# A softmax-plus-feed-forward kernel: two output tiles finished before either is copied, two batches' states transposed by TensorE at the start, and one batch's M sessions moved up

## The chip, the cores and the metric

The kernel runs on one core of one Trainium2 chip. The metric is device time in microseconds (us) of one execution, lower is better. TensorE is called PE below, VectorE DVE, ScalarE ACT, GpSimd POOL and SyncE SP.

## What is computed

There are 8 batches, each with 8 heads, 512 tokens and 32 state rows, and 64 elements per head. An attention goes both ways between tokens and state, and its result goes through a feed-forward layer:

```
B, H, S, Ns, D = 8, 8, 512, 32, 64          # x: B,H,S,D   state: B,H,Ns,D
scores  = x @ state^T / sqrt(D);   a  = softmax(scores);    xread = a  @ state
scores2 = state @ x^T / sqrt(D);   a2 = softmax(scores2);   sread = a2 @ x
rows = concat([xread, sread], axis=2) -> transposed to (B * 544, 512)
h = rows @ w_in                       # 512 x 2048
out = max(0.01 * h, h) @ w_out        # 2048 x 512, result 4352 x 512, float32
```

## The kernel before, in words

The order of instructions on every engine is written out by hand: what the program says in order is what each engine runs in order, and an instruction that waits holds all that stand behind it on its engine. SP's queue is one such order too: it issues loads, stores and the transposing DMAs.

**The work of one batch.** `xread @ w_in` is not formed in two steps. The kernel multiplies the state with `w_in` first (`a_m`, line 334: "M sessions", four per batch, each for 512 of the 2048 columns; `m_evict`, lines 346 and 348, copies a session from PSUM into the bf16 tile `M`) and then multiplies the probabilities `aT` with `M` (`ff1`, line 355, 16 steps of two matmuls, each followed by the leaky ReLU on ACT, line 360, into `hT`). The second layer is cut into "pieces" (`piece`, line 383): a piece is four of the 16 matmuls that make an output tile of 128 tokens. Four pieces (`jq` 0 to 3) finish a tile, and there are four tiles (`i`) to a batch. The last piece is followed by a copy out of PSUM into `ysb` (line 389) and a store on SP's queue (line 395).

**The attention of one batch.** `a_scores` (line 213) makes the scores in PSUM (tag `sc`). `a_shift` (DVE, lines 223 to 233) finds the maximum over the 32 state rows and gives `sh`; `a_exp` (ACT, line 240) the exponentials; `a_probs` (DVE, lines 245 to 255) the sums, reciprocals and `aT`. `a_max2`, `a_exp2`, `a_probs2` (lines 273 to 292) do the other softmax, over tokens, and `a_a2t` transposes its result by a DMA on SP (line 299), which `a_sread` (line 307) needs.

**Transposes.** PE needs x and state with the head's elements on partitions. x of batches 0 to 2 is transposed by PE (lines 434 and 193), later batches by a DMA (`a_xt_dma`, line 185). The states of batches 0 and 1 are transposed at the start by eight small matmuls against an identity (`state01`, line 146). Those of batches 2 to 7 are loaded by eight DMAs (`load_state`, line 165), cast by POOL (line 171) and transposed by one DMA (line 172).

**The stretch around the change.** Batch 0 is the start: its loads, scores, M sessions and ff1 are written out one by one. `spin` runs matmuls on zeros. Then comes batch 0's second layer (lines 612 to 642), and between its pieces stands all that batch 1 needs before its own ff1: the transposes of x (lines 616 to 619), scores, M sessions 1 to 3, both softmaxes. Tiles 0 and 1 lie in two PSUM banks of their own (tag `py`); tiles 2 and 3 share one PSUM tile of two banks, `wide` (named `pyw`). Tiles 2 and 3 are finished here, tiles 0 and 1 in the first steps of batch 1's ff1. After that a loop of 16 steps `s` (line 655) runs batch 1's ff1 with pieces between, and holds batch 2's attention; a second loop (line 688) does batches 2 to 7 in the same manner, each with the next batch's attention inside.

PSUM tiles are handed out by tag; a tag's next user waits until the last reader of the tile before is done. DMAs on SP share eight counters in turn, so each waits for the one eight places before it.

Of the kernel before, what the change touches and what calls it, by code (L numbers as in the profile page):

```python
# [9 lines left out]
P = 128  # L10
# [17 lines left out]
def kernel(  # L28
# [34 lines left out]
    xv = x[0].rearrange("h (p t) d -> p h (t d)", t=NT)  # L63
    for u in range(2):
        nc.sync.dma_start(xf[u][:], xv[:, NK * u:NK * (u + 1)])
    idle = consts.tile([P, S], BF16, name="idle")
    nc.vector.memset(idle[:], 0.0)
    warm = consts.tile([P, 2], FP32, name="warm")
# [58 lines left out]
    def spin(n, tag):  # L127
        p = psum.tile([P, S], FP32, name="pspin", tag=tag, bufs=2 if tag in ("ph", "py") else 1)
        for _ in range(n):
            nc.tensor.matmul(p[:], lhsT=idle[:, :P], rhs=idle[:], start=True, stop=True)  # L130
# [3 lines left out]

    stbd = consts.tile([P, NK, 2, NS], BF16, name="stbd")
    st1 = consts.tile([P, P], BF16, name="st1")
    st_t = consts.tile([P, B - 2, P], BF16, name="st_t")
    sr_t = consts.tile([P, NK, B * NS], BF16, name="sr_t")

    stb0 = consts.tile([P, 4, D], BF16, name="stb0")  # L140
# [15 lines left out]
            ps[:, :, D:].rearrange("p r (k q) -> p k q r", q=8),  # L156
        )

    stf = consts.tile([P, B - 2, P], FP32, name="stf")
    stb = consts.tile([P, B - 2, P], BF16, name="stb")  # L160

    def load_state():
        for k in range(NK):
            for g in range(2):
                nc.sync.dma_start(
                    stf[NS * k:NS * (k + 1), :, D * g:D * (g + 1)],
                    state[2:, 2 * k + g].rearrange("b n d -> n b d"),
                )

    def state_t():  # L170
        POO(stb[:], stf[:])
        nc.sync.dma_start_transpose(st_t[:], stb[:].rearrange("p b q -> p (b q)"))
# [30 lines left out]
    def st_of(a, g, k):  # L203
        rows = slice(D * g, D * (g + 1))
        if a.b == 0:
            return stbd[rows, k, g ^ (k // 2), :]
        return (st1 if a.b == 1 else st_t[:, a.b - 2])[rows, NS * k:NS * (k + 1)]

    def a_scores(a):
        sc = psum.tile([P, 2, S], FP32, name="sc", tag="sc", bufs=1)  # L210
        for k in range(NK):
            for g in range(2):
                nc.tensor.matmul(  # L213
                    sc[NS * k:NS * (k + 1), g, :],
                    lhsT=st_of(a, g, k),
                    rhs=a.xT[D * g:D * (g + 1), :, k, :],
                    start=True, stop=True,
                )
        a.sc = sc
# [44 lines left out]
    def a_exp(a):  # L264
        a.e1 = block_exp(a.sh, NB)
# [76 lines left out]
    def m_evict(a, c, pm, copy):  # L342
        cols = slice(DM * c, DM * (c + 1))
        if isinstance(pm, list):
            for g in range(2):
                copy(a.M[:, g, cols], pm[g][:])  # L346
        else:
            copy(a.M[:, :, cols], pm[:])  # L348
# [28 lines left out]
    def piece(b, hT, i, jq, bank=None, copy=SCA):  # L377
        if jq == 0:
            y = ys[b, i] = Y()
            y.py = psum.tile([P, DM], FP32, name="py", tag="py")[:] if bank is None else bank  # L380
        y = ys[b, i]
        for j in range(4 * jq, 4 * jq + 4):
            nc.tensor.matmul(  # L383
                y.py, lhsT=hT[:, j, P * i:P * (i + 1)], rhs=w_out_bf[:, j, :],
                start=(j == 0), stop=(j == 15),
            )
        if jq == 3:
            ysb = ypool.tile([P, DM], FP32, name="ysb", tag="ysb")
            copy(ysb[:], y.py)  # L389
            if b == B:  # L390
                for bb in range(4):
                    r0 = (4 * i + bb) * SROW + S
                    nc.sync.dma_start(out[r0:r0 + NS, :], ysb[NS * bb:NS * (bb + 1), :])  # L393
            else:
                nc.sync.dma_start(rows_of(b)[i], ysb[:])

    def rows_of(b):
        return out[b * SROW:b * SROW + S, :].rearrange("(p t) f -> t p f", t=NT)
# [40 lines left out]
    def xt0_evict(u, pxt, copies):  # L439
        for v, copy in enumerate(copies):  # L440
            copy(a0.xT[:, :, 2 * u + v, :], pxt[v][:])
# [16 lines left out]
    def rows0(u):  # L458
        scn[u] = psum.tile([P, S], FP32, name="scn", tag="ph")
        for c in range(NK):  # L460
            nc.tensor.matmul(
                scn[u][NS * c:NS * (c + 1), :], lhsT=stbd[:, 2 * u + c // 2, c % 2, :],
                rhs=a0.xT[:, :, 2 * u + c // 2, :], start=True, stop=False,
            )
# [70 lines left out]
    pxt = x0_half(1)  # L535
    m = max0(0)
    xt0_evict(1, pxt, (SCA, VEC))
    rows0(0)
    m = split0(m)
    scores0(1)  # L540
# [1 line left out]
    rows0(1)  # L542
    spread0(scn[0], m[0], False)
    exp0(0)
    spin(2, "py")
    spread0(scn[1], split0(m[1]), False)
    exp0(1)
    sum0(0)
# [63 lines left out]
    for i in (0, 1):  # L612
        piece(0, h0, i, 0)
    wide = psum.tile([P, 2, DM], FP32, name="pyw", tag="big", bufs=1)
    piece(0, h0, 2, 0, bank=wide[:, 0])
    for t0, copy in ((0, VEC), (2, SCA)):
        ps = psum.tile([P, 2, NK, P], BF16, name="pxt2", tag="ph")
        a_xt_pe(a1, ps, t0, t0 + 2)
        copy(a1.xT[:, t0:t0 + 2], ps[:])
    piece(0, h0, 3, 0, bank=wide[:, 1])  # L620
    nc.vector.memset(stf[:, 0, D - 1:D + 1], 0.0)
    load_state()
    a_scores(a1)
    m_evict(a1, 1, a_m(a1, 1, "ph"), SCA)
    a_shift(a1)
    a_max2(a1)
    for i in range(NT):
        piece(0, h0, i, 1)
        if i in (1, 3):
            c = 2 + i // 2  # L630
            m_evict(a1, c, a_m(a1, c, "ph"), SCA)
    a_exp(a1)
    for g in range(2):
        a_exp2(a1, g)
    a_probs(a1)
    state_t()
    open_xb(2)
    cast_x(2, 0, 8, SCA)
    for i in range(NT):
        piece(0, h0, i, 2)  # L640
    for i in (2, 3):
        piece(0, h0, i, 3, copy=VEC)
    a_probs2(a0)
    a_a2t(a0)
    a_probs2(a1)
    a_a2t(a1)
    a_open(a2, 2)


# [5 lines left out]
    for s in range(16):  # L655
        ff1(a1, h1, s)
        if s % 2:
            pb, hT, i, jq = fill[s // 2]
            piece(pb, hT, i, jq, copy=VEC if s == 3 else SCA)
        if s == 2:  # L660
            a_xt_full(a2)
            VEC(a2.xT[:], a2.pxt[:])
        elif s == 4:
            a_scores(a2)
            m_evict(a2, 0, a_m(a2, 0, "big"), SCA)
            a_shift(a2)
            a_max2(a2)
            cast_x(3, 0, 8, POO)
        elif s == 8:
            a_exp(a2)  # L670
        elif s == 9:
            a_sread(a0)
        elif s in (10, 11):
            a_exp2(a2, s - 10)
            if s == 11:
                a_probs(a2)
                a_probs2(a2)
        elif s == 13:
            pm = [a_m(a2, 1, "big"), a_m(a2, 2, "sc")]
            m_evict(a2, 1, pm[0], VEC)  # L680
            m_evict(a2, 2, pm[1], SCA)
            a_open(att_of[3], 3)
            a_xt_dma(att_of[3])
# [4 lines left out]
    for b in range(2, B):  # L688
        hT = hpool.tile([P, 16, S], BF16, name="hT", tag="hT")
        a = att_of[b]  # L690
        nxt = att_of[b + 1] if b + 1 < B else None
        order = [(b - 1, i, 3) for i in range(2)]
        order += [(b - 1, i, jq) for i in range(2, NT) for jq in range(4)]
        order += [(b, i, jq) for jq in range(3) for i in range(2)]
        for s in range(16):
            ff1(a, hT, s)
            if s == 0:
                if b + 2 < B:
                    load_x(b + 2, nc.sync)
                    open_xb(b + 2)  # L700
                a_a2t(a)
            elif s == 1:
                if nxt is not None:
                    a_scores(nxt)
                m_evict(a, 3, a_m(a, 3, "big"), SCA)
                if nxt is not None:
                    a_shift(nxt)
                    a_max2(nxt)
                if b + 2 < B:
                    cast_x(b + 2, 0, 8, POO)  # L710
            elif s == 6:
                if b == 2:
                    a_sread(a1)
            elif s == 8:
                a_sread(a)
            if nxt is not None:
                if s == 5:
                    a_exp(nxt)
                elif s in (6, 7):
                    a_exp2(nxt, s - 6)  # L720
                    if s == 7:
                        a_probs(nxt)
                        a_probs2(nxt)
                elif s == 10:
                    pm0 = a_m(nxt, 0, "big")
                    pm2 = a_m(nxt, 2, "phpy")
                    pm1 = a_m(nxt, 1, "sc")
                    m_evict(nxt, 2, pm2, VEC)
                    m_evict(nxt, 0, pm0, VEC)
                    m_evict(nxt, 1, pm1, SCA)  # L730
                if s == 13 and b + 2 < B:
                    a_open(att_of[b + 2], b + 2)
                    a_xt_dma(att_of[b + 2])
            pb, i, jq = order[s]
            piece(pb, hT if pb == b else h_prev, i, jq)
        h_prev = hT
# [48 lines left out]
```

## Time and profile before

| | us |
|---|---|
| median of three timed runs | 220.35 (220.31, 220.35, 222.07) |
| profiled execution: time | 222.05 |
| profiled execution: span from first to last instruction | 220.2 |

| engine | busy us | share of span |
|---|---|---|
| PE (matmul) | 211.4 | 96% |
| ACT | 139.3 | 63% |
| DVE | 100.2 | 45% |
| PE weight loads (beside matmuls) | 98.9 | 45% |
| POOL | 22.3 | 10% |

The profile is of one execution. Its page gives the busy time of each engine, the span in 40 slices, a chain of waits from the end backwards, and groups of instructions by line; the trace behind it gives every instruction with start, length and what ended the idle time before it. "Lnnn" is a line of the kernel before. The mean granted PE clock is 0.992 of full speed. The granted clock of a stretch is part of its row in a table of windows.

### The profile page before, as it was taken

How to read it: one execution, taken by the hardware profiler on the slowest of the kernel's cores; microseconds unless marked ns; L12 is line 12 of the kernel's file. 1: busy time of each engine (PE TensorE's matmuls, PEld its weight loads, DVE VectorE, ACT ScalarE, POOL GpSimd, SP SyncE). 2: the span in 40 equal slices, each digit the busy share in tenths (PEclk: the TensorE clock that was granted, in tenths of full speed). 3: DMA queues.
4: the chain of work that ended last, by engine and by line, in shares of the span. 5: the costliest groups of instructions: out<-in, count | busy, mean ns of one | idle time of the engine just before them, and what ended most of it. 6: DMA issues, size and time to landing. Idle time of an engine off the chain costs nothing.

```text
span 220.2 us, 3735 instructions
## 1 busy us (share of the span) xinstructions
PE 211.4 (96%) x1524; PEld 98.9 (45%) x1524; DVE 100.2 (45%) x152; ACT 139.3 (63%) x261; POOL 22.3 (10%) x36
## 2 busy tenths in 40 slices
PE   7999995999999999999999999999999999999993
PEld 2533432444345444444444444444444445466653
DVE  1676388489696607670667146733674000000000
ACT  3469757378869647874778477857685665554420
POOL 8820201003030003000300030000000000000000
PEclk9999999699999999999999999999999999999999
DMA  5999993695931395139512951181114111111113
GB/s 188 218 206 293 207 288 37 163 224 169 271 119 48 86 259 135 48 79 246 153 41 59 233 151 47 68 172 51 48 48 98 44 52 48 51 40 55 48 44 102
DMA packets 37632, 27.17 MB, mean 123 GB/s; under 512 B 22256, under 2 KB 32880, under 8 KB 37616
## 3 DMA queue, kind: packets, MB, share of 16 engines
q1 hardware_dynamic: 32704, 20.52, 35.6%
q0 software_dynamic: 4768, 6.29, 14.2%
q8 instruction: 12, 0.20, 0.4%
q10 hardware_dynamic: 144, 0.13, 0.3%
q14 instruction: 4, 0.03, 0.1%
HBM read 17.30 MB, written 8.91 MB: 119 GB/s over the span
## 4 chain that ended last, share of the span: by engine, by line
PE 78%; DMA 10%; ACT 4%; SPq 2%; DVE 2%; POOL 1%; issue 1%; ACTq 0%; POOLq 0%
PE py L383 46%; PE ph L355 22%; DMA xl<-in_x_dram 7%; PE pm L334 3%; PE ph L366 3%; DMA xf<-in_x_dram 3%; SPq L393 2%; PE psr L307 1%; PE pyw L383 1%; PE sc L213 1%; ACT hT L360 1%; ACT e L240 1%; PE pxt L193 1%; DMA out_dram<-ysb 1%; DVE qb L254 1%; DVE r L245 1%
## 5 line engine op out<-in xcount | busy, mean ns | idle before, releaser
L383 PE MATMUL py<-w_out_bf,hT 128*128 128x512 bf16 x464 | 119.4, 381 | 0.0
L360 ACT ACTIVATE hT<-ph 128x512 bf16<-128x512 f32 x112 | 67.0, 601 | 45.5 <-PE ph L355 45.5
L383 PEld LDWEIGHTS <-hT 128*128 128x128 bf16 x496 | 47.0, 98 | 61.0 <-issue 9.5
L355 PE MATMUL ph<-aT,M 128*128 128x512 bf16 x224 | 66.8, 384 | 0.3 <-ACT hT L360 0.3
L355 PEld LDWEIGHTS <-M 128*128 128x128 bf16 x224 | 21.8, 99 | 27.5 <-issue 2.7
L389 ACT COPY ysb<-py 128x512 f32<-128x512 f32 x30 | 17.6, 586 | 11.2 <-PE py L383 11.2
L223 DVE TRANSPOSE_TENSOR_REDUCE mrow<-sc 128x32 f32<-128x1024 f32 x7 | 8.8, 1250 | 32.9 <-PE sc L213 32.7
L411 DVE COPY ysh<-pyh 128x256 f32<-128x256 f32 x1 | 0.4, 424 | 47.7 <-PE pyh L406 47.7
L103 POOL CAST xb<-xl 128x2048 bf16<-128x2048 f32 (+1 forms) x6 | 10.6, 1766 | 93.8 <-DMA xl<-in_x_dram 44.4
L348 ACT CAST M<-pm 128x1024 bf16<-128x1024 f32 x13 | 13.2, 1013 | 1.1 <-PE pm L334 0.6
L245 DVE TRANSPOSE_TENSOR_REDUCE r<-e 128x32 f32<-128x1024 bf16 x7 | 8.7, 1243 | 11.1 <-ACT e L240 11.1
L348 DVE CAST M<-pm 128x1024 bf16<-128x1024 f32 x9 | 10.9, 1217 | 1.5 <-PE pm L334 1.5
L281 ACT ACTIVATE e<-sc,mcols 128x512 bf16<-128x512 f32 x16 | 11.1, 698 | 0.0
L383 PE MATMUL pyw<-w_out_bf,hT 128*128 128x512 bf16 x32 | 8.0, 386 | 2.8 <-DVE ysb L389 2.8
L346 DVE CAST M<-pm 128x512 bf16<-128x512 f32 x12 | 7.7, 685 | 6.3 <-PE pm L334 6.3
L273 DVE TENSOR_REDUCE mcol<-sc 128x2 f32<-128x1024 f32 x8 | 9.7, 1213 | 0.0
L370 ACT ACTIVATE hs<-ph 128x256 bf16<-128x256 f32 x16 | 6.0, 384 | 4.6 <-PE ph L366 4.4
L231 DVE STREAM_TRANSPOSE mrowb<-mrow 128x1024 f32<-128x1024 f32 x7 | 8.7, 1245 | 0.2
L254 DVE STREAM_TRANSPOSE qb<-qh 128x1024 bf16<-128x1024 bf16 x7 | 8.7, 1245 | 0.2
L233 DVE TENSOR_TENSOR sh<-sc,mrowb 128x1024 f32<-128x1024 f32 x7 | 8.6, 1224 | 0.2
L366 PE MATMUL ph<-sr_t,w_in_bf 128*128 128x256 bf16 x64 | 8.3, 273 | 0.0
L582 ACT ACTIVATE hT<-ph 128x512 bf16<-128x512 f32 x12 | 6.4, 598 | 2.1 <-PE ph L574 2.0
(98 smaller groups left out, 158.4 us busy)
## 6 DMA issues: line engine op xcount, KB each, us to landing
out_dram<-ysb SPq DMA_DIRECT2D x31, 256.0 KB, 2.3
xl<-in_x_dram SPq DMA_DIRECT2D x5, 1024.0 KB, 6.8
w_in_bf<-in_moe_w_in_dram POOLq DMA_DIRECT2D x4, 512.0 KB, 8.7
w_out_bf<-in_moe_w_out_dram POOLq DMA_DIRECT2D x4, 512.0 KB, 17.4
xl<-in_x_dram POOLq DMA_DIRECT2D x2, 1024.0 KB, 19.2
xf<-in_x_dram SPq DMA_DIRECT2D x2, 512.0 KB, 5.1
out_dram<-ysb SPq DMA_DIRECT2D x8, 64.0 KB, 1.7
stf<-in_state_dram SPq DMA_DIRECT2D x8, 48.0 KB, 8.0
```

Source lines behind the costliest of these rows:

```text
L103: copy(xs[b][:, :, h0:h1].rearrange("p t h d -> p h t d"), xl[b][:, h0:h1].rearrange("p h (t d) -> p h t d", t=NT),)
L223: nc.vector.tensor_reduce(out=m1[:], in_=flat.rearrange("p (c j) -> p c j", j=NS), axis=AX.X, op=ALU.max, apply_transpose=True,)
L245: nc.vector.tensor_reduce(out=r1[:], in_=e1[:].rearrange("p (c j) -> p c j", j=NS), axis=AX.X, op=ALU.add, apply_transpose=True,)
L254: nc.vector.transpose(q1b[:], q1h[:, :, None].to_broadcast([P, n, NS]))
L273: nc.vector.tensor_reduce(out=m2[:], in_=a.sc[:], axis=AX.X, op=ALU.max, negate=True)
L281: nc.scalar.activation(out=a.e2[:, g], in_=a.sc[:, g, :], func=AF.Exp, bias=a.m2s[:, g:g + 1], scale=SCALE, accum_out=a.r2[:, g:g + 1],)
L348: copy(a.M[:, :, cols], pm[:])
L355: nc.tensor.matmul(ph[:], lhsT=a.M[:, g, P * j:P * (j + 1)], rhs=a.aT[:, g, :], start=(g == 0), stop=(g == 1),)
L360: nc.scalar.activation(out=hT[:, j, :], in_=ph[:], func=AF.Prelu, alpha=0.01)
L366: nc.tensor.matmul(ph[:, :n], lhsT=w_in_bf[:, k, P * j:P * (j + 1)], rhs=sr_t[:, k, :], start=(k == 0), stop=(k == NK - 1),)
L383: nc.tensor.matmul(y.py, lhsT=hT[:, j, P * i:P * (i + 1)], rhs=w_out_bf[:, j, :], start=(j == 0), stop=(j == 15),)
L389: copy(ysb[:], y.py)
```

## The change

1. `state23`: one load of 128 KB brings the states of batches 2 and 3 in at the start, behind the two loads of batch 0's x on SP. ACT casts them. Eight small matmuls against the identity, in the place of `spin(2)`, and one ACT copy make `st23`. `load_state` and `state_t` then cover batches 4 to 7; the eight loads move from batch 0's second layer to step 6 of batch 1's loop, and the cast and the transposing DMA to step 4 of batch 2's. A memset on `stf` goes.
2. In batch 0's second layer, tile 3's first piece comes ahead of batch 1's transposes, the scores come after the first piece of the second round, and M sessions 1 to 3 follow the first three pieces of that round one by one.
3. Tiles 2 and 3 are both finished, then both copied and stored (`y_store`).
4. Batch 1's token softmax is finished (`a_probs2`, `a_a2t`) at step 8 of its loop and no longer ahead of it. In that loop batch 2's `a_exp2` are at steps 10 and 12 (were 10 and 11), `a_probs` at 10, `a_probs2` at 12 (were 11), its M sessions 1 and 2 and batch 3's transposing DMA at 14 (were 13).

```diff
+    st2f = consts.tile([P, 4, D], FP32, name="st2f")
+    nc.sync.dma_start(
+        st2f[:], state[2:4].rearrange("b h n d -> (b h n) d").rearrange("(p r) d -> p r d", r=4)
+    )
...
+    stb2 = consts.tile([P, 4, D], BF16, name="stb2")
+
+    def state23():
+        ps = psum.tile([P, 4, D], FP32, name="pst2", tag="sc", bufs=1)
+        for r in range(4):
+            for g in range(2):
+                nc.tensor.matmul(
+                    ps[D * g:D * (g + 1), r, :].rearrange("p (c q) -> p c q", q=8),
+                    lhsT=stb2[:, r, :],
+                    rhs=ident[:].rearrange("p (c v q) -> p c v q", v=2, q=8)[:, :, g],
+                    start=True, stop=True,
+                )
+        SCA(
+            st23[:].rearrange("p b (k q r) -> p (b k) q r", k=NK, r=4),
+            ps[:].rearrange("p r (c q) -> p c q r", q=8),
+        )
...
-                    state[2:, 2 * k + g].rearrange("b n d -> n b d"),
+                    state[4:, 2 * k + g].rearrange("b n d -> n b d"),
...
-        if jq == 3:
-            ysb = ypool.tile([P, DM], FP32, name="ysb", tag="ysb")
-            copy(ysb[:], y.py)
...
+        if jq == 3 and copy is not None:
+            y_store(b, i, copy)
+
+    def y_store(b, i, copy):
+        ysb = ypool.tile([P, DM], FP32, name="ysb", tag="ysb")
+        copy(ysb[:], ys[b, i].py)
...
     xt0_evict(1, pxt, (SCA, VEC))
+    SCA(stb2[:], st2f[:])
     rows0(0)
...
     exp0(0)
-    spin(2, "py")
+    state23()
     spread0(scn[1], split0(m[1]), False)
...
     wide = psum.tile([P, 2, DM], FP32, name="pyw", tag="big", bufs=1)
-    piece(0, h0, 2, 0, bank=wide[:, 0])
+    for i in (2, 3):
+        piece(0, h0, i, 0, bank=wide[:, i - 2])
     for t0, copy in ((0, VEC), (2, SCA)):
...
-    piece(0, h0, 3, 0, bank=wide[:, 1])
-    nc.vector.memset(stf[:, 0, D - 1:D + 1], 0.0)
-    load_state()
-    a_scores(a1)
-    m_evict(a1, 1, a_m(a1, 1, "ph"), SCA)
+    for i in range(NT):
+        piece(0, h0, i, 1)
+        if i == 0:
+            a_scores(a1)
+        if i < 3:
+            m_evict(a1, 1 + i, a_m(a1, 1 + i, "ph"), SCA)
     a_shift(a1)
     a_max2(a1)
-    for i in range(NT):
-        piece(0, h0, i, 1)
-        if i in (1, 3):
-            c = 2 + i // 2
-            m_evict(a1, c, a_m(a1, c, "ph"), SCA)
     a_exp(a1)
...
     a_probs(a1)
-    state_t()
...
     for i in (2, 3):
-        piece(0, h0, i, 3, copy=VEC)
+        piece(0, h0, i, 3, copy=None)
+    for i in (2, 3):
+        y_store(0, i, VEC)
     a_probs2(a0)
     a_a2t(a0)
-    a_probs2(a1)
-    a_a2t(a1)
     a_open(a2, 2)
...
+        elif s == 6:
+            load_state()
         elif s == 8:
             a_exp(a2)
+            a_probs2(a1)
+            a_a2t(a1)
         elif s == 9:
             a_sread(a0)
-        elif s in (10, 11):
-            a_exp2(a2, s - 10)
-            if s == 11:
-                a_probs(a2)
-                a_probs2(a2)
-        elif s == 13:
+        elif s == 10:
+            a_exp2(a2, 0)
+            a_probs(a2)
+        elif s == 12:
+            a_exp2(a2, 1)
+            a_probs2(a2)
+        elif s == 14:
             pm = [a_m(a2, 1, "big"), a_m(a2, 2, "sc")]
...
+            elif s == 4:
+                if b == 2:
+                    state_t()
```

More of the change, by code (lines that the diff above doesn't have):

```diff
@@ L136 @@
     st1 = consts.tile([P, P], BF16, name="st1")
-    st_t = consts.tile([P, B - 2, P], BF16, name="st_t")
+    st23 = consts.tile([P, 2, P], BF16, name="st23")
+    st_t = consts.tile([P, B - 4, P], BF16, name="st_t")
     sr_t = consts.tile([P, NK, B * NS], BF16, name="sr_t")
@@ L157, in state01 @@
         )
-    stf = consts.tile([P, B - 2, P], FP32, name="stf")
-    stb = consts.tile([P, B - 2, P], BF16, name="stb")
+    stb2 = consts.tile([P, 4, D], BF16, name="stb2")
[13 more added lines that the diff above has]
+        )
+    stf = consts.tile([P, B - 4, P], FP32, name="stf")
+    stb = consts.tile([P, B - 4, P], BF16, name="stb")
     def load_state():
@@ L206, in st_of @@
             return stbd[rows, k, g ^ (k // 2), :]
-        return (st1 if a.b == 1 else st_t[:, a.b - 2])[rows, NS * k:NS * (k + 1)]
+        t = st1 if a.b == 1 else st23[:, a.b - 2] if a.b < 4 else st_t[:, a.b - 4]
+        return t[rows, NS * k:NS * (k + 1)]
     def a_scores(a):
@@ L386, in piece @@
             )
-        if jq == 3:
-            ysb = ypool.tile([P, DM], FP32, name="ysb", tag="ysb")
[L389 to L395, printed above, removed]
+        if jq == 3 and copy is not None:
[3 more added lines that the diff above has]
+        copy(ysb[:], ys[b, i].py)
+        if b == B:
+            for bb in range(4):
+                r0 = (4 * i + bb) * SROW + S
+                nc.sync.dma_start(out[r0:r0 + NS, :], ysb[NS * bb:NS * (bb + 1), :])
+        else:
+            nc.sync.dma_start(rows_of(b)[i], ysb[:])
     def rows_of(b):
```

## The prediction

> **What bounds the kernel now.** I read the page's slices first, then the windows around the one dip, then the chain of waits, then the engines' order of time there.
>
> The busy slices of PE and of its clock (page, part 2; a slice is 5.5 us):
>
> ```profile
> PE   7999995999999999999999999999999999999993
> ...
> PEclk9999999699999999999999999999999999999999
> ```
>
> PE is full except at both ends and in slice seven (33.0 to 38.5 us), and the slice behind that one has the only low clock. Windows of 3.4 us around it (columns: length, busy us and count of PE, weight loads, DVE, ACT, POOL, then granted clock, DMA share, GB/s):
>
> ```profile
> 32.70:36.10 3.40, 3.40 (x16) 1.46 (x15) 2.20 (x4) 3.22 (x7) 0.00 (x0) 1.00 0.64 74
> 36.10:39.50 3.40, 0.64 (x3) 0.29 (x3) 2.67 (x3) 1.07 (x1) 0.83 (x1) 1.00 0.15 31
> 39.50:42.90 3.40, 3.40 (x10) 1.20 (x9) 2.40 (x9) 1.19 (x2) 0.00 (x0) 0.50 0.57 183
> 42.90:46.30 3.40, 3.40 (x34) 1.92 (x33) 1.57 (x2) 1.68 (x3) 0.00 (x0) 0.99 1.09 182
> ```
>
> PE did 0.64 us of work in one window and was given half the clock in the next: 10 matmuls where its neighbours have 31 to 34. The waits list has one long wait of PE:
>
> ```profile
> PE pyw L383 <- DVE ysb L389: 2.8, 1, 2.8
> ```
>
> All other waits of PE together are some 2.8 us, 1.2 of them before its first instruction. In order of time (start, length, engine):
>
> ```profile
> 31.74 1.07 ACT L346 CAST M<-pm 128x512 bf16<-128x512 f32 x2 [1.10 <-PE pm L334]
> 32.69 1.07 ACT L240 ACTIVATE e<-sh 128x1024 bf16<-128x1024 f32 x1
> 33.80 1.25 DVE L245 TRANSPOSE_TENSOR_REDUCE r<-e 128x32 f32<-128x1024 bf16 x1 [1.50 <-ACT e L240]
> 36.84 0.83 POOL L171 CAST stb<-stf 128x768 bf16<-128x768 f32 x1 [12.19 <-DMA stf<-in_state_dram]
> 36.96 1.25 DVE L255 TENSOR_TENSOR aT<-e,qb 128x1024 bf16<-128x1024 bf16 x1
> 38.13 0.68 DVE L389 COPY ysb<-pyw 128x512 f32<-128x512 f32 x1
> 38.86 1.24 PE L383 MATMUL pyw<-w_out_bf,hT 128*128 128x512 bf16 x4 [2.77 <-DVE ysb L389]
> 39.90 1.92 PE L355 MATMUL ph<-aT,M 128*128 128x512 bf16 x4
> ```
>
> Tile 3's last quarter (38.86) writes the PSUM tile that the copy of tile 2 reads, and that copy stands on DVE behind batch 1's softmax. Even without this, ff1 of batch 1 (39.90) needs aT, ready at 38.21. So aT is the second lock on the same door. It is late because the third M eviction (31.74) holds ACT before the exponential, though `sh` was ready at 30.97, and because aT took 1.25 beside POOL's cast (other batches 0.69).
>
> **The change, part by part.** Times are those of this execution (222.05 us, its span 220.2 plus 1.85).
>
> *States in the head.* A 128 KB load goes onto SP behind the two xf loads. Those let DVE start at 5.44 and 6.83, so 512 KB take 1.4 us, and 128 KB 0.35: landed at 7.2, or 7.6 if it shares with w_in. ACT casts it after its xT copy (7.77 + 0.58 = 8.35); a 128x256 cast from PSUM took 0.37 (L150), so 8.72. PE wants it at 9.69, where the two spins stood. Eight small matmuls took 0.46 from start to next (L146), so 10.15; PE waits there anyway, for `hi`, until 10.22. The ACT copy of `st23` (0.37) fits between the exponentials at 9.81 to 10.41 and 10.96, and is over (10.78) when the M session at 11.02 writes the same PSUM tag. Cost nothing; with the cover gone every tenth costs a tenth, since the head is one chain. Bounds: 0 and 0.5. The load also pushes POOL's queue back by some 0.35: batch 1's x lands at 23.8 instead of 23.46.
>
> *Fourth tile's first quarter ahead of the transposes.* PE starts its 16 matmuls at 21.71; at 0.216 each the transposes follow at 25.17 (before 24.30), so the later x (casts over by 25.0) is covered. They end at 26.2, ACT's xT copy (1.01) runs 26.3 to 27.3, scores start at 27.35 (before 26.70): the softmax chain starts 0.65 later, `sh` ready at 31.65.
>
> *M sessions moved up.* Session 1 follows the scores (matmuls end 28.0), its two ACT copies take 1.07, to 29.15. Session 2 comes after one piece (0.86) and needs both ph banks, so PE waits about 0.4; session 3 likewise. Copies end at 30.75 and 32.3. The exponential then starts at 32.3 and not 31.65: the third eviction still holds it, though less than before (32.69). End 33.4, sums start 33.45. From there to aT's start the rows give 3.16 (33.80 to 36.96) and aT itself 0.69, since the cast that it met has moved: aT at 37.3.
>
> PE meanwhile: 27.35, 0.56 for scores and session, three pieces with two sessions and their waits to 32.0, then four quarters and twice one quarter, 24 matmuls or 5.2 us: 37.15. The two tiles end without a wait between them and ff1 starts at **37.35 instead of 39.90: 2.55 saved**. The waits of 0.25 and twice 0.4 are inside this.
>
> *Both copies after both tiles.* Twice 0.69 on DVE behind aT: 38.75. Behind them stand a0's second probabilities (1.0, to 39.75) and the copy of xT for batch 2. PE needs the PSUM tile again at 39.5 (37.35 + 0.43 + 1.29 + 0.43), 0.7 after the copies: covered.
>
> *The half clock.* From 39.90 to 42.95 PE worked at 0.43 per matmul instead of 0.216. That is 1.52 lost, all of it after a gap of 2.77. With idle pieces of 0.4 at most it should not come: **1.52 saved**. Here the timed runs help: 220.31, 220.35 and 222.07 differ by 1.72, which is half of 3.41. I take it that the first two ran without the dip, so of this term the median holds nothing.
>
> The Trainium skill (TensorE: Matmul & The Clock Gate, Part 1) puts this to a free-running window of 3413 ns, so the cost depends on where the gap falls in it, and it asks for an idle window, or a gap over about 3 us. The 3.41 agrees with this trace. The gap here was only 2.77; by the letter that is too short, the dip has another cause and stays, and the sum would be 1.52 higher.
>
> *Fill slots of batch 1.* Spreading batch 2's column exponentials over s = 10 and 12 should remove the one wait left for ACT (0.30 before 54.79): **0.30 saved**. Against it: second probabilities of a1 (1.0) now stand on DVE between batch 2's maxima and sums. Their cover before was the idle time at 40 us; now it is batch 2's slack. And the x of batch 3 comes earlier: its load follows only one transpose on SP, issue 41.15 (before 44.50), landed after the same 6.3 at 47.3, so POOL casts from 47.3 to 49.2. What that does is seen here:
>
> ```profile
> 50.84 1.89 POOL L103 CAST xb<-xl 128x2048 bf16<-128x2048 f32 x1 [13.18 <-DMA xl<-in_x_dram]
> ...
> 51.71 1.05 DVE L275 TENSOR_SCALAR mcols<-mcol 128x2 f32<-128x2 f32 x1
> 52.67 1.23 DVE L245 TRANSPOSE_TENSOR_REDUCE r<-e 128x32 f32<-128x1024 bf16 x1
> 52.76 1.78 SPq L185 DMA_TRANSPOSE xT<-xb  x1
> ```
>
> mcols (0.17 elsewhere) ended with the cast. In the changed kernel mcols comes up at 47.6 and is held to 49.2; between 0 and 1.9 late, I take 1.6. Then a1's probabilities to 50.25, and aT of batch 2 after 3.85 at 54.1. Before, PE came for it (batch 2's first ff1) at 58.47; now at 58.47 - 2.55 - 1.52 - 0.30 = 54.1: no wait, and nothing to spare. On SP a1's transpose goes out at 50.3 (1.3) and only behind it xT of batch 3, at 51.65; landed 4.4 later (median of part 6): 56.05. Scores of batch 3 come up at 55.9 (before 60.29) and the eviction that frees the next PSUM tile ends at 56.4. I charge **0.40**, between 0 and 1.5.
>
> *State load moved to s = 6, cast and transpose to batch 2.* Eight issues on SP (3.85 before), the last three of which wait in the queue until batch 3's x has landed (they share its counters), are over at 49. Cast and transpose are wanted by batch 4's scores, some 20 us on: nothing on the path. POOL's cast stands behind batch 4's x.
>
> Sum: 222.05 - 2.55 - 1.52 - 0.30 + 0.40 = 218.08. From the other end: 220.33 less 2.37 (without the dip ff1 starts at 39.72 before) less 0.30 plus 0.40 gives 218.1. After this PE is full to its last instruction, so nothing gives it back.
>
> **Rivals.**
> A. *aT stays where it was.* The M sessions crowd ACT and the exponential starts no sooner than before; ff1 waits until 38.3. For: exp waits for the third eviction in my own schedule, and the chain starts 0.65 later. Against: three evictions end at 32.3, and aT is 0.56 shorter. 219.0.
> B. *The timed runs carry the dip too* and differ for another reason; then all 3.97 come off 220.35: 216.4. For: one profile only shows the clock. Against: 1.72 is so near half of 3.41.
> C. *A half-clock window remains*, from the small waits between 27 and 31 us or because the spins of the head are gone. For: 1.05 us idle within 4. Against: from 10.4 to 13.8 PE was busy 3.00 of 3.40, in small matmuls, and kept 1.00. 218.1 + 1.5 = 219.6. A dip with another cause than the gap, as the Trainium skill's page would have it by the letter, ends here as well.
> D. *Slower: xT of batch 3 arrives late.* It stands on SP behind eight state loads and a1's transpose. If the loads need the 8.0 of part 6 to land, a1's transpose, which shares a counter with the first, goes out at 52; if its issue takes 2.75 as the one at 78.03, xT goes out at 54.8, and with 5.1 to landing (as at 74.25) is there at 59.9. PE stands 4.0 at batch 3's scores: 218.1 + 3.65 = 221.75, and a half-clock window behind such a gap makes 223.4. It decides from 58.6 on: there the gain is gone. Against: before, xT had 3.2 us to spare.
>
> **How the numbers follow.** Forecast 0.54, A 0.14, B 0.14, C 0.06, D 0.12. The likeliest gives 218.1. The measurement tells about 1% from nothing, here 218.15 and 222.55. The forecast's own range, 217.3 to 219.0, lies across the first; I give 0.32 to faster, since a before with the dip in it helps, and 0.22 to same. Faster: 0.32 + 0.14 = 0.46. Slower: half of D, 0.06. Same: the rest, 0.48. The range goes from B to half-way into D, 216.3 to 220.2, and leaves out most of D.
>
> **What would show it.** Right: no PE gap over 0.5 between 36 and 40; ff1 of batch 1 at 37.0 to 37.7; no clock of 0.50; aT 0.69 long; batch 3's scores at 56 to 57. Wrong: ff1 after 38 (A), a 0.50 window (C), a PE gap over 1.5 before batch 3's scores (D).

## The result: 219.7 us, a quarter of the forecast gain

| | before | after |
|---|---|---|
| median of 20 executions, us | 220.47 (219.97 to 222.07) | 219.70 (219.35 to 220.09) |
| ratio of means | | 0.9948, 95% interval 0.9930 to 0.9967 |
| profiled execution: time, span | 222.05, 220.2 | 220.09, 218.0 |

The changed kernel is faster by about half a per cent. The executions of before fall into two groups, 13 of them from 219.97 to 220.71 (mean 220.27) and 7 from 221.71 to 222.07 (mean 221.87). Those of after form one group. A ratio of means therefore depends on how often the slower kind of before turns up. Where half a microsecond matters below, medians are set against 220.3, the level of before without the half-clock window.

In the page of after, the dip in slice seven is gone from PE and from its clock. The digits 7, 7 and 8 in front are the head, and the 8 in slice eleven (54.5 to 60.0) is a wait that is read below:

```profile
PE   7789999999899999999999999999999999999993
PEclk9999999999999999999999999999999999999999
```

The windows around the old gap (length, busy us and count of PE, weight loads, DVE, ACT, POOL, granted clock, DMA share, GB/s) are full and at full clock:

```profile
36.10:39.50 3.40, 3.40 (x17) 1.45 (x16) 3.15 (x5) 1.94 (x3) 0.00 (x0) 1.00 0.00 0
39.50:42.90 3.40, 3.40 (x29) 1.86 (x26) 2.37 (x6) 1.96 (x4) 0.00 (x0) 1.00 0.87 212
```

In order of time, aT takes 0.69 as forecast, the copies of tiles 2 and 3 run after it in one go, and ff1 of batch 1 (L378, which was L355) follows the last piece directly:

```profile
37.30 0.69 DVE L278 TENSOR_TENSOR aT<-e,qb 128x1024 bf16<-128x1024 bf16 x1
38.05 1.04 PE L378 MATMUL ph<-aT,M 128*128 128x512 bf16 x4
38.21 1.29 DVE L415 COPY ysb<-pyw 128x512 f32<-128x512 f32 x2 [0.21 <-PE pyw L406]
```

So the door that the change is about is open. What PE now waits for, by the waits list of after:

```profile
PE pspin L134 <- DVE warm L73: 1.2, 1, 1.2
PE sc L236 <- DMA xT<-xb: 1.0, 1, 1.0
PE pm L357 <- DMA w_in_bf<-in_moe_w_in_dram: 0.6, 1, 0.6
PE pxth L460 <- DVE xb L114: 0.5, 1, 0.5
PE ph L378 <- ACT hT L383: 0.3, 1, 0.3
```

The second, the third and the fourth are new. The third is in the head: PE's M session for the next 512 columns stood 0.60 until 15.82 for the third chunk of `w_in`. The fourth is there too, but cost little: PE was free earlier than in before, and the transposes that waited for DVE's cast began at 6.02 and not 5.92. The second is the scores of batch 3, whose x comes by the transposing DMA (in the rows, `a<-e,qc` makes the probabilities of batch 1's token softmax, and `a2T<-a` is their transpose, called a1's below):

```profile
43.71 7.11 SPq L187 DMA_DIRECT2D stf<-in_state_dram  x8
...
48.84 0.61 DVE L315 TENSOR_SCALAR a<-e,qc 128x512 bf16<-128x512 bf16 x2
...
49.23 1.98 POOL L107 CAST xb<-xl 128x2048 bf16<-128x2048 f32 x1 [24.03 <-DMA xl<-in_x_dram]
...
50.92 1.24 SPq L322 DMA_TRANSPOSE a2T<-a  x1
...
52.27 3.49 SPq L207 DMA_TRANSPOSE xT<-xb  x1
...
58.02 0.41 PE L236 MATMUL sc<-xT,st 64*32 64x512 bf16 x8 [1.01 <-DMA xT<-xb]
```

xT went out at 52.27, took 3.49 only to be issued (1.78 before), and landed at 57.98, 5.7 after it went out (4.3 before). Ahead of it, the cast ended at 51.2. a1's transpose went out at 50.92, right behind the eight state loads, which held SP until 50.82, though its probabilities were ready at 49.45; it was issued in 1.24.

The lead of after over before, in the two profiled executions, at five points of PE's order:

| PE reaches | before | after | lead | forecast lead |
|---|---|---|---|---|
| second layer of batch 0 | 21.71 | 22.61 | -0.90 | 0 |
| ff1 of batch 1 | 39.90 | 38.05 | 1.85 | 2.55 |
| scores of batch 2 (behind the half clock) | 46.28 | 42.93 | 3.35 | 4.07 |
| scores of batch 3 | 60.29 | 58.02 | 2.27 | 3.97 |
| last PE instruction | 216.93 | 214.67 | 2.26 | 3.97 |

### The profile page after: what moved, and what is told of

Read it like the earlier page. It is cut to its first block, busy times and chain, and to the rows that moved or that the text cites. A ratio compares the mean times of both kernels' runs of the same rounds, so it can differ in the third digit from the quotient of the medians.

```text
span 218.0 us, 3745 instructions
## 1 busy us (share of the span) xinstructions
PE 209.7 (96%) x1530; PEld 98.5 (45%) x1530; DVE 100.2 (46%) x151; ACT 139.9 (64%) x263; POOL 22.2 (10%) x36
## 3 DMA queue, kind: packets, MB, share of 16 engines
q0 software_dynamic: 4768, 6.29, 14.2%
## 4 chain that ended last, share of the span: by engine, by line
PE 82%; DMA 8%; DVE 4%; POOL 2%; ACT 1%; SPq 1%; issue 1%; POOLq 0%; ACTq 0%
PE py L406 47%; PE ph L378 20%; DMA w_in_bf<-in_moe_w_in_dram 5%; PE pm L357 4%; PE pyw L406 3%; PE ph L389 3%; DMA xT<-xb 3%; PE ph L601 2%; PE psr L330 1%; PE sc L236 1%; PE pxt L215 1%; DMA out_dram<-ysb 1%; POOL w_in_bf L120 1%; DVE mrow L246 1%; DVE mrowb L254 1%; DVE M L371 1%
## 5 line engine op out<-in xcount | busy, mean ns | idle before, releaser
L378 PE MATMUL ph<-aT,M 128*128 128x512 bf16 x224 | 66.1, 379 | 0.3 <-ACT hT L383 0.3
L378 PEld LDWEIGHTS <-M 128*128 128x128 bf16 x224 | 21.6, 98 | 27.0 <-issue 1.6
```

Source lines behind the costliest of these rows:

```text
L378: nc.tensor.matmul(ph[:], lhsT=a.M[:, g, P * j:P * (j + 1)], rhs=a.aT[:, g, :], start=(g == 0), stop=(g == 1),)
```

## Experiments

Two questions stand out. Where do the 0.9 in the head and the late xT come from? And what do the timed executions of before hold of the half clock? The theory on xT (I, formed on the trace) is this: PE's own instructions arrive by DMA, in blocks of 16 KB, and in the changed kernel one such block arrives while batch 3's transposing DMA is under way. The page of after has the blocks among its DMA queues (queue and kind, packets, MB, share of the DMA engines):

```profile
q8 instruction: 12, 0.20, 0.4%
```

The same page counts 1530 matmuls and 1530 weight loads, which makes some 255 to a block. The block in question is the fourth of the 12 in each trace; the expectations and the table below call it the sixth. The 256-byte packets of the transposes, counted from the trace by the microsecond in which they start:

```
packets of 256 bytes, started in        52   53   54   55   56   57   longest
after  (16 KB block at 54.27, 0.93 long) 721  676  126   31 1125  393   1.99 us
e7     (16 KB block at 50.41, 1.20 long) 259  726  797  841  451    0   0.17 us
```

In after the transpose nearly stops for two microseconds, just when the block comes: the 21 packets that are held all end between 55.99 and 56.03, 0.8 after the block's end at 55.20. Before, the block came at 60.32, when xT had long landed. The rival Q is that SP's queue does it: a1's transpose, the eight state loads and the x of batch 3 stand ahead of xT there.

**Before, again.** The kernel before, unchanged, for the two groups.

> The kernel before, unchanged, to see the granted clock beside each run's time. Theory (the two groups of times, about 220.2 and 221.9, differ by one half-clock window of 3.41 us): the runs near 220.2 have a mean clock of 0.999 or 1.000, those near 221.9 have 0.992 (0.5 x 3.41 / 220 = 0.008 missing). Rival (the dip is in all runs and the groups have another cause): 0.992 in all.

Of 12 executions, 7 had a mean granted clock of 0.991 to 0.992 and took 221.59 to 222.35 (mean 221.89); 5 had 0.999 to 1.0 and took 220.14 to 220.65 (mean 220.32). The half-clock window is there in about half of the executions and costs 1.57. Rival B of the prediction falls, and so does the sentence that the median holds nothing of this term: it holds it or not by chance.

**The load alone.** Before, with the 128 KB load of the states added and nothing that reads it.

```diff
+    st2f = consts.tile([P, 4, D], FP32, name="st2f")
+    nc.sync.dma_start(st2f[:], state[2:4]...)
```

> The kernel before with the 128 KB load of two batches' states added behind the two loads of x on SP; nothing reads it. Theory (the load pushes the weights back and the head starts late): third chunk of w_in lands near 15.8 and PE waits for it some 0.6 us; first matmul of the second layer (L387) near 22.6 and not 21.7; time up by 0.5 to 0.9, about 220.9. Rival (the head is late for another reason, ACT's added work or the spins that are gone): first matmul of the second layer at 21.7 to 21.9, time 220.2 as before.

Second layer at 22.33, a wait of 0.61 for `w_in`'s third chunk (landed 15.50). The median, 222.1, says little, since 7 of 10 executions carry the window. Group against group of the executions of before beside it, the load costs 0.13 without the window (mean 220.47 of three, against 220.34) and 0.30 with it (222.24 of seven, against 221.94): less than the 0.5 to 0.9 expected. Over all kernels of this study, one profiled execution each, the second layer starts at a mean of 21.95 without the load in the head (ten kernels) and 22.46 with it (four). The chunk itself lands between 14.2 and 15.4 without the load, and between 15.5 and 15.8 with it. With such a spread a single profile says little here.

**Copies alone.** Before, with only the copies and stores of tiles 2 and 3 put behind both tiles.

```diff
     for i in (2, 3):
-        piece(0, h0, i, 3, copy=VEC)
+        piece(0, h0, i, 3, copy=None)
+    for i in (2, 3):
+        y_store(0, i, VEC)
```

> The kernel before with only the two copies put behind both tiles. Theory (aT is the second lock, ready at 38.2): PE runs on to 37.0, waits 1.2 to 1.3 us, ff1 of batch 1 starts at 38.3; that is 1.4 to 1.6 less than before, and the idle window is gone, so no half clock: 218.7 with every run near it. Rival (the copies were all of it): ff1 at 37.0, 217.4. Other rival (a wait of 1.3 still drops the clock in some runs): two groups of times, 1.7 apart.

219.55 (218.59 to 219.89), ratio 0.9927 (0.9898 to 0.9955), no execution of ten with the window. Two lines of the change give as much as all of it. ff1 waits for aT, as the prediction's second lock said, in PE's timeline:

```profile
38.08 1.04 PE L355 MATMUL ph<-aT,M 128*128 128x512 bf16 x4 [1.09 <-DVE aT L255]
```

In ten executions an idle stretch of some 1.1 did not bring the half clock. But batch 3's scores wait 0.68 for xT here too, with the states as before and no state load near: the block came at 55.67 and xT took 6.2. Here no packet of 256 bytes took over 0.15 before the landing. Late were the last two of the 4-byte packets that follow the data: they started at 56.62 and 56.63, when the block ended (56.63).

**Copies and M sessions.** The same with parts 2 and 3 of the change whole; the states stay as before.

> The changed kernel's order of pieces, copies and M sessions in batch 0's second layer, with the states of batches 2 to 7 loaded and transposed as before, so without the load in the head. Theory (head late by 0.9 through the load; sessions moved up bring aT forward): second layer starts at 21.7; aT is held by POOL's state cast until 37.7 and ready near 37.8; ff1 at 37.9; no half clock; batch 3's transpose of x lands in time (no wait over 0.3 before its scores): 218.2. Rival (moving the sessions brings nothing, ACT holds the exponential as before): ff1 at 38.3 or later, 218.7 or more. If the head's load is not what cost 0.9, second layer starts near 22.6 here too and the time is 219.2.

219.12 (218.6 to 219.75), ratio 0.9919 (0.9891 to 0.9947). Second layer 21.74, ff1 37.17 without a wait: the prediction's 37.35 for this part holds. The hold of aT by POOL's cast, which the expectation of 37.9 rests on, did not come: aT took 0.69 and was ready at 37.11. The expected 218.2 was missed by 0.9 all the same; PE waited 1.01 for xT (block at 53.93, xT 5.35).

**States later.** The changed kernel, with the states of batches 2 and 3 loaded at about 27 us and transposed in step 1 of batch 1's loop.

```diff
-    state23()
+    spin(2, "py")
...
-        if s == 2:
+        if s == 1:
+            state23()
+        elif s == 2:
```

> The changed kernel with the load of batches 2's and 3's states sent only after batch 1's transposes (near 27 us), its cast behind batch 2's on ACT, the eight matmuls at step 1 of batch 1's loop, and the two spins back in the head. Theory (the load in the head costs 0.2 to 0.6 there, the rest of the 0.9 is the weights' third chunk meeting a 16 KB instruction load): second layer starts at 21.7 to 22.1 and not 22.6, ff1 of batch 1 at 37.2 to 37.6, 0.3 lost again at step 1; batch 3's scores still near 57 to 58, since its x is not earlier: time 219.1 to 219.7, little better. Rival (the head was what kept the gain back): 218.7 or less.

219.81 (219.12 to 220.21): no gain, and a little above the 219.1 to 219.7 expected. Second layer 22.26, so the head kept part of its lateness in this execution, for another reason: PE did not wait for `w_in`, but DVE's second cast of batch 0's x started behind POOL's and took 0.77 (0.43 in before). This doesn't settle the load's price; the moved work has one of its own in the loop.

**State loads later.** The changed kernel, with `load_state` at step 3 and `state_t` at step 11 of batch 2, so that nothing of them stands ahead of xT.

> The changed kernel with the eight state loads moved from step 6 of batch 1's loop to step 3 of batch 2's, cast and transpose to step 11, so that nothing stands on SP ahead of a1's transpose and that of batch 3's x. Theory Q (the queue made x late): a1's transpose goes out at 49.5, x's at 51.3, landed by 55.7; no wait before batch 3's scores, 1.0 saved: 218.7. Theory I (a 16 KB instruction load near 54.3 holds up the transpose's packets for 1.4 to 2.0 us wherever it meets them): x goes out at 51.3 and lands at 57 or later all the same, PE waits 0.5 to 1.0, time 219.3 to 219.7.

219.36 (218.86 to 219.81), and xT still took 5.25 (52.24 to 57.49), with the block at 53.82; PE waited 0.82. With nothing of the states ahead of it the DMA is still long, so Q falls as the cause of that. Whether the queue also sends xT out late, this run can't tell: a1's transpose was expected at 49.5 and went out at 50.90, as in after, but now because its probabilities met POOL's cast, a collision that the prediction had put at `mcols`. In the timeline of this run:

```profile
48.54 2.33 DVE L315 TENSOR_SCALAR a<-e,qc 128x512 bf16<-128x512 bf16 x2
...
48.84 1.89 POOL L107 CAST xb<-xl 128x2048 bf16<-128x2048 f32 x1 [24.02 <-DMA xl<-in_x_dram]
...
50.90 1.24 SPq L322 DMA_TRANSPOSE a2T<-a  x1
```

The two steps of L315 took 0.61 in after (48.84, ahead of the cast at 49.23). Here they meet POOL's cast and take 2.33. The median is 0.34 below after's, but most of that lies outside the span, which is 217.6 in the median of both.

**Cut matmuls.** The changed kernel, with 24 matmuls of batch 0's second layer written as two halves of 256 columns. The arithmetic is the same; PE has 48 more instructions (matmuls and weight loads), so the block is due earlier.

```diff
-            nc.tensor.matmul(y.py, lhsT=hT[...], rhs=w_out_bf[:, j, :], ...)
+            for q in range(2 if cut else 1):
+                cols = slice(256 * q, 256 * (q + 1)) if cut else slice(0, DM)
+                nc.tensor.matmul(y.py[:, cols], lhsT=hT[...], rhs=w_out_bf[:, j, cols], ...)
```

> The changed kernel with 24 of the 512-column matmuls of batch 0's second layer each cut into two of 256 columns: the same PE work in 48 more instructions, so PE's instruction loads (16 KB each) come some 3 us earlier against the work. SP's queue is as in the changed kernel. Theory I: the load comes near 51 and not in the middle of the transpose of batch 3's x, which goes out at 52.3 as before and lands 4.3 to 4.5 later, at 56.7; the wait before batch 3's scores falls from 1.0 to 0.2 or less: 219.0. Theory Q: the wait stays at 1.0, time 219.7 or a little more through the cut matmuls.

219.03 (218.64 to 219.99), 0.67 below after. The block came at 50.41, xT landed 4.4 after it went out, and the wait shrank to 0.31 (expected: 0.2 or less):

```profile
52.83 2.08 SPq L207 DMA_TRANSPOSE xT<-xb  x1
```
```profile
57.30 0.41 PE L236 MATMUL sc<-xT,st 64*32 64x512 bf16 x8 [0.31 <-DMA xT<-xb]
```

**Copies and M sessions, cut.** The version with parts 2 and 3 of the change, and 20 matmuls cut.

> The order of pieces, copies and M sessions of the change with states as before, and 20 matmuls cut in halves (40 more PE instructions). Theory I: the instruction load moves from 53.9 to some 51.3, between the stores and the transpose of batch 3's x, which lands at 56.1 instead of 57.1; the wait of 1.0 before batch 3's scores is gone: 218.0 to 218.2, the fastest so far. Theory Q has no state loads on SP here to blame; by it the wait was the x load's own time, and stays: 219.0.

218.57 (218.53 to 218.64), ratio 0.9891 (0.9838 to 0.9945): the fastest version, below both kernels. The block came at 52.37 and not at 51.3; it met only the early packets of xT (4.9 to landing), and PE did not wait for xT. The expected 218.0 to 218.2 was missed: in the profiled execution aT took 1.17 beside POOL's state cast, and ff1 waited 0.34 for it, until 37.98. The rows of xT and of the scores:

```profile
51.48 3.02 SPq L185 DMA_TRANSPOSE xT<-xb  x1
```
```profile
56.88 0.41 PE L213 MATMUL sc<-xT,st_t 64*32 64x512 bf16 x8
```

**Copies alone, cut.** 20 matmuls cut in the version with only the copies apart.

> The kernel before with only the copies put behind both tiles, and with 20 matmuls of the second layer written in halves. Theory I: the sixth instruction load comes some 1.5 to 3 us earlier than 55.67, batch 3's transposing DMA lands 4.5 to 5 after its issue, and the wait of 0.68 before batch 3's scores is gone or under 0.2. The added instructions cost nothing, since PE stood 1.09 before ff1 of batch 1 anyway and that shrinks to about 0.7: ff1 again at 38.1, time 218.9 (from 219.55). If the moved M sessions are worth their 0.6 to 0.9 once the transpose is in time, this one stays 0.2 to 0.5 above the 218.57 of the version that has them; if not, both give the same.

218.87 (218.68 to 219.25), as expected; block at 52.57, xT 4.6, no wait before batch 3's scores, ff1 at 38.24. That is 0.68 less than the same without the cuts, and 0.30 more than with the M sessions.

**Before, cut: 32, 20 and 24.** The test in the other direction: put a block into the transpose of the kernel before, where PE has some 3 us to spare.

> The kernel before with 32 of batch 0's second-layer matmuls (pieces of the second and third round, tiles 0 to 3: 16 quarters' worth of them) written as two halves of 256 columns each, so that PE has more instructions ahead of batch 3's transpose and the same arithmetic. Theory I (an instruction load of 16 KB stalls the transposing DMA that it meets): the sixth load moves from 60.3 to about 55 and falls into batch 3's transposing DMA, which then takes 5.2 to 6.2 from issue to landing and not 4.3. PE does not notice, since this DMA has some 3 us to spare in the kernel before: time within 0.5 of the kernel before. Rival Q (the long landing in the changed kernel comes of what stands ahead on the queue there, not of the load): landing stays at 4.3 to 4.5.

> The kernel before with 20 matmuls of batch 0's second layer written in halves (the version with 32 moved the sixth load from 60.3 to 51.57, 0.6 ahead of batch 3's transposing DMA, so it missed it). 64 more PE instructions, one per matmul and one per weight load, moved it by some 7 in an execution without the half-clock window (58.7 to 51.6), so 40 should move it by 4.4: to 54.3 without that window, 56.1 with it. Theory I: it falls into batch 3's transposing DMA, which takes 5.2 to 6.2 from issue to landing. Rival Q: 4.3 to 4.5 as before. PE: no wait before batch 3's scores in either case, time as before.

> The kernel before with 24 matmuls of batch 0's second layer written in halves. With 20 the sixth load came at 57.24 (with the half-clock window), near the end of batch 3's transposing DMA (53.08 to 57.93, 4.85); with 32 it came at 51.57 (without that window), ahead of it (4.36). With 24 it should come at about 54.2 without the window and 55.9 with it, in the middle of the DMA either way. Theory I: 5.2 to 6.2 from issue to landing, packets of 256 bytes of 1 us and more beside the load. Rival Q: 4.3 to 4.5, no such packets before the landing. No wait before batch 3's scores over 0.3 in either case, since this kernel has 2 to 3 us to spare there.

With 32 the block came at 51.57 and ended at 52.78, ahead of xT's first packet (53.36): the test missed its target, and xT took 4.36. The time was that of before (220.95, ratio 1.0009, 0.9971 to 1.0047), so the cuts in themselves save nothing. With 20 it came at 57.24, just as the last 4-byte packets started, and xT took 4.85 and not the 5.2 to 6.2 expected. With 24 it came at 57.26, later than expected, among the last packets, and xT took 6.2:

```profile
53.09 1.86 SPq L185 DMA_TRANSPOSE xT<-xb  x1
```
```profile
60.06 0.41 PE L213 MATMUL sc<-xT,st_t 64*32 64x512 bf16 x8
```

It landed at 59.30, so PE, at 60.06, had nothing to wait for. No packet of 256 bytes took 1 us before the landing here; eight such packets started after 57.0, and the last two of the 4-byte packets that follow them at 58.18 and 58.19, when the block ended (58.19). The expected mark of long packets failed, the late landing came. Both versions ran once, with the half-clock window: 221.87 and 221.83, the level of before with it. All runs together:

```
xT of batch 3:          out    sixth block   landed   out to landing   PE's wait
before                  52.76  60.32         57.08    4.3              0
e0 before, again        53.27  60.67         57.64    4.4              0
e1 load alone           53.16  60.82         57.54    4.4              0
e10 before, 32 cut      52.17  51.57         56.53    4.4              0
e7 after, 24 cut        52.83  50.41         57.26    4.4              0.31
e11 copies, 20 cut      51.63  52.57         56.23    4.6              0
e12 before, 20 cut      53.08  57.24         57.93    4.9              0
e9 sessions, 20 cut     51.48  52.37         56.39    4.9              0
e5 loads later          52.24  53.82         57.49    5.2              0.82
e4 states late          52.30  53.44         57.62    5.3              0.66
e3 sessions             51.75  53.93         57.10    5.4              1.01
after                   52.27  54.27         57.98    5.7              1.01
e2 copies               51.48  55.67         57.69    6.2              0.68
e13 before, 24 cut      53.09  57.26         59.30    6.2              0
```

The five where the block stayed clear of the DMA's packets are the five at 4.3 to 4.4. In the six where packets of 256 bytes were held (after, e3, e4, e5, e9, e11), the last of them ended 0.7 to 0.9 after the block's end.

The later batches say the same. These 14 traces hold 70 transposes of x. The 51 that no block met between going out and landing took 4.25 to 4.50. The 19 that one met took 4.36 to 6.22, and only two of them under 4.6: there the block had ended before the first packet.

## Why the prediction was wrong

*What held.* ff1 is freed by putting the copies behind both tiles, aT is the second lock, and moving the M sessions opens it: from the second layer to ff1 the prediction gave 15.64, and after shows 15.44, the version with parts 2 and 3 alone 15.43; the 0.2 that the prediction adds between 37.15 and 37.35 did not come. aT is 0.69 long. No execution of any kernel without the long gap had a half-clock window (80 executions of after and seven variants, mean granted clock 0.997 or more), so rival C falls. Rival A's 38.3 comes near the measured 38.05, but for another reason: aT ended at 37.99, just ahead of PE, and both are late by what the head lost.

*The step that failed most: the 0.40 for batch 3's scores.* The prediction looked for the lateness in POOL's cast holding `mcols` (1.6 late) and in the queue. x landed at 49.17 and not at 47.3, mcols took 0.17, and xT went out at 52.27, 0.6 after the forecast 51.65; that much is the queue, since the state loads were over at 50.8 and not at 49. The rest is the DMA itself: 5.7 where the prediction took the median 4.4. With 4.4, xT would have landed at 56.7, and PE, who came at 57.0, would not have waited. The wait was 1.01. Moving the block away gave back 0.67, 0.55 and 0.68 in the medians of three pairs (after and e7, e3 and e9, e2 and e11). Rival D had the right place and, but for those 0.6, the wrong cause: with the state loads out of the way the DMA still took 5.25. What the prediction lacked was a count of PE's instructions. A sign was in its own trace: the transpose that went out at 74.25, whose 5.1 rival D quotes, met the block of 74.16, and the other four there took 4.3 to 4.5 and met none. And the trace of before had the block at 60.32, 3.2 behind xT's landing, and the change brought the block forward by 6.05 and xT's issue by only 0.5.

*The head, "cost nothing", bounds 0 and 0.5.* 0.90 late in the profiled execution: 0.60 of it is the wait for `w_in`'s third chunk. The means over the profiled executions give 0.5 for the kernels with the load. In medians, the kernels with the states' part stand 0.58 above the one without it (219.70 and 219.12), and 0.46 with the block out of the way (219.03 and 218.57; e7's remaining wait for xT is 0.31). Of these, 0.27 and 0.24 lie outside the span: the time less the span is 2.07 on average in after and e7, 1.80 in e3 and 1.83 in e9. Inside it the states' part costs 0.2 to 0.3 (median spans 217.6 and 217.35, 216.95 and 216.75). Why the time outside differs, no run shows; e5 has the states' part too, and 1.79. The value of nothing was wrong, and the bound of 0.5 was passed in the profiled execution. What share the load has in it stays open, since taking the states out of the head gave nothing.

*The 0.30 for ACT.* Not saved: in after, ff1 waits the same 0.30 for `hT` at 51.44. Spreading the column exponentials over two more steps did not move what ACT does ahead of that step.

*The half clock, 1.52.* The size was right (1.57 between the groups, 1.50 in the lead from ff1 to batch 2's scores). What the median of before holds of it was taken as nothing from three times; in 20 times it is there in 7.

*The sum.* Profiled executions: forecast 3.97 less, measured 1.96. The 2.01 between are 0.70 at ff1, 0.30 for ACT, 0.68 at batch 3's scores (1.08 of the lead lost there for a charge of 0.40), 0.26 in what lies around the span (2.07 and not 1.81; the other kernels show 1.8 or 2.07, too), and 0.07 in small steps. In medians, from 220.3: forecast 2.2 less, measured 0.6; 0.6 of the difference is xT beyond its charge, 0.5 the states with what lies outside the span, 0.3 ACT, and 0.2 stays unassigned.

## What to carry to other kernels

Ahead of moving PE forward, list what has to arrive by then, and price a DMA with little slack by its longest landing in the trace, not by its median. Count PE's instructions to the place: a change that adds or removes some dozens shifts every later instruction load by microseconds, and cutting a few matmuls in halves can move one out of a critical transfer. Try the smallest edit alone; here two lines out of four parts gave all the measured gain, and the versions with the states' part (after, e7) are slower than those without it (e3, e9).

## What the runs showed of the hardware that I had not expected

**Instruction loads reach the data.** Each of the 12 blocks of an execution is one packet of 16 KB that takes 0.9 to 1.8 us on a DMA engine where a transposing DMA's 256-byte packets take 0.02. A transpose that meets one lands up to 1.9 later (4.3 to 6.2 above), and its issue on SP grew from 1.8 to 3.5 in after. No wait of PE that the profile lists is for its instructions. Why packets that started up to 0.25 before the block are held too, and some until 0.8 after its end, no run shows. The Trainium skill (Runtime: NRT & Kernel Launch, section "Instruction fetch mechanics") says that a sequencer refills its instruction memory in blocks of 16 KiB, 256 instructions, over a DMA queue of its own, and that crossing a block is mostly hidden. The size and the count agree with the trace. "Hidden" holds for PE's sequencer here, and not for the transfer that shares the engines. Packets of 256 bytes of 1.0 to 1.4 us also occur where no PE block is near (at 60.5, in batch 2's a2T, of the kernels before with 20 and with 24 cut), so this is one cause of such stalls and not the only one, though no transpose of x was late without a block.

**A gap shorter than a window brings the half clock.** The granted clock in the windows of before with 20 matmuls cut (PE idle 2.38, 36.32 to 38.70), and then of before with 32 cut (idle 2.27):

```profile
36.10:39.50 3.40, 1.02 (x4) 0.25 (x2) 2.51 (x3) 1.00 (x1) 0.83 (x1) 0.88 0.21 41
39.50:42.90 3.40, 3.40 (x11) 1.33 (x10) 2.16 (x9) 1.19 (x2) 0.00 (x0) 0.62 0.51 169
```
```profile
36.10:39.50 3.40, 1.13 (x6) 0.44 (x5) 2.40 (x3) 0.97 (x1) 0.83 (x1) 1.00 0.24 48
39.50:42.90 3.40, 3.40 (x29) 2.01 (x28) 2.61 (x10) 2.17 (x4) 0.00 (x0) 1.00 0.60 191
```

A mean of 0.88 is 0.82 us at half clock, and 0.62 is 2.58: together 3.40, so the slow stretch ran from 38.68 to 42.08. The clock's own records in the trace agree (half clock for 3.41 from 38.70), and in before they have full clock for 34.13 from 5.40 on, ten times 3.41, and then half for 3.41: the windows follow one another without a break. The 3.40 ahead of the slow stretch that starts at 38.70 had 1.04 of work in them, so a window need not be idle throughout. The second kernel had the slow stretch in 5 of its 10 executions, though not in this one. An estimate: if the slow stretch follows a fixed window of 3.40 with at least T of idle time, a gap of 2.7 at a random place gives it in (3.40 + 2.7 - 2T) / 3.40 of the executions; 43 in 97 of before puts T at 2.3, and 5 in 10 with the gap of 2.27 at 2.0. The traces agree: by their clock records the gap put 2.38 to 2.74 of idle time into one window in the five with the slow stretch, and 1.78 in the one without it. The longest gap that never brought it was 1.09 in the profiled execution. The Trainium skill (TensorE: Matmul & The Clock Gate, Part 1) has the free-running window of 3413 ns, which agrees, and asks for an idle one, which does not.
